# Second layer's value sums with the values as 32-column weights, in a kernel ordered by a planner

## The chip, the cores and the metric

The kernel runs on one core of one Trainium2 chip. The metric is device time in microseconds (us) of one launch. The kernel before takes 1893.77 us (median of 3 runs, 1893.45 to 1894.54).

A core has five engines with queues of their own: PE (matrix multiplication; it reads weights and a moving operand from SBUF and writes PSUM), ACT (ScalarE, here above all exponentials), DVE (VectorE), POOL (GpSimd) and SP (SyncE, here issuing the DMAs). PSUM has 8 banks of 512 f32 columns in 128 partitions.

## The reference

Four layers are applied to x of 2048 tokens by 512 features. Each layer normalizes x, makes Q, K and V with 32 heads of 16 features, attends, and adds the projected result to x. The layers are called first to fourth; in the code they are L = 0 to 3. The first and third (kind A) share one set of weights, the second and fourth (kind B) another.

```python
x = A_x
x = x + _A_ref(_layernorm(x, axis=-1), A_wq, A_wk, A_wv, A_wo, A_beta)
x = x + _B_ref(_layernorm(x, axis=-1), B_wqkv, B_wo)
x = x + _A_ref(_layernorm(x, axis=-1), A_wq, A_wk, A_wv, A_wo, A_beta)
x = x + _B_ref(_layernorm(x, axis=-1), B_wqkv, B_wo)
```

Kind A cuts the tokens into 4 segments of 512. Within a segment it is causal softmax attention; between segments a memory matrix M (a sum of phi(k) v over earlier segments) adds a linear term, mixed by a gate. Kind B is full softmax attention over all 2048 tokens:

```python
scores = jnp.einsum('bhqd,bhkd->bhqk', q, k) * Dh ** (-0.5)
p = _softmax(scores, axis=-1)
o = jnp.einsum('bhqk,bhkd->bhqd', p, v)
```

The softmax runs without subtracting a maximum; the sum of the exponentials comes from a column of ones beside V.

## The kernel before

Work is cut into groups. A group is one layer, one segment of 512 queries (`qseg`), one block of 128 features (`c`, 4 of them) and one parity of heads (`e`), so it holds 4 heads, one in each 32-partition row of the array (r = 0..3); the queries are masked so that only 16 of a row's 32 features count (`qm`). A group's scores come in banks: 128 keys by 512 queries of one head, on a 32-row tile of PE. A full group of kind B has 16 key tiles x 4 heads = 64 banks. A group of kind A has 12 causal ones, worth 10 banks' width.

A unit of work (`unit`, main loop in `attention`) is up to three banks of scores on PE, one ACT instruction that turns them into exp in SBUF (`pT`, line 1349), and the value sums of an earlier unit (`pv`). Units alternate between PSUM banks 0 to 2 and 4 to 6; bank 3 (`DXB`) is for projections and spare scores, bank 7 (`ACC`) is the one accumulator of value sums.

Some banks of kind B go to DVE instead of ACT (`dx_*`): one instruction from PSUM writes a piecewise approximation of exp as 16-bit integers (line 980), three more add constants to it in SBUF (line 1032), and all four copies are summed by PE. So a bank on DVE has four value sums where a bank on ACT has one. `dx_room` decides whether a unit may take some; the copies live in 9 buffers (`dxw`) and in tiles that are free by then (`dx_areas`: four in QA and VA while the second layer's full groups run, and up to 34 in weights, keys and others later).

Value sums have two forms. In the first the exponentials are the weights: 128 keys by 128 queries are loaded, 17 columns of V (16 and the ones) move through, four times for a bank. In the second (`g.fm`) the 17 columns of V are the weights, in a 32-column tile of the array that belongs to the head's row, and the bank's 512 exponentials move through once. `FM` says which groups take the second form (line 264): 1 is the last layer's full groups, 2 all of the last layer, 3 also the second layer's full groups, 4 all of kind B. At the end of a group (`finish`) the first form takes a reciprocal and a product and sends the output to SP's transposing DMA; the second (`finish_fm`) first transposes the accumulator on DVE in 32x32 blocks, then takes reciprocal and product, and for each pair of groups transposes back on DVE. Its temporary tiles are the upper half of KA.

Where keys aren't complete yet, kind B runs partial groups: in the second layer segment 0's queries against each key segment as it comes (32 groups), in the fourth against two segments and again two (`split` cuts the last ones further). Their sums are kept in f32 in free key or value tiles (`accS`).

Everything else (norms, projections, phi, memory, output projections) is a task, a generator that yields between pieces. `ORDER` is each task's priority: for layer pair and segment the keys of task_A, task_phi, task_mem, task_B and task_out. `background` and `bg_one` fit pieces in between units by credits.

The order of all instructions is fixed when the program is built. `Sched` keeps an estimated time for each engine; `Sched.estimate` prices each instruction, a PE instruction by its columns and by how its tile of the array stands to the last twelve. Most class constants of `Builder` (CR_*, DQ, NEAR_*, GAP and so on) are limits on such estimates. `select` chooses the next pair of groups: with `ALT` 1 it goes over to kind B after each pair of the third layer's first two segments. `keep_busy` adds matmuls on zeros where the estimate finds PE too idle.

The start: `setup` issues the input DMAs on SP and 66 warming matmuls; `ln_part` takes mean and variance of four tiles on DVE and an inverse root by two Newton steps; `ln_first` normalizes, transposes on PE and evacuates; then `task_A` projects K and Q of the first block, `select` masks Q from the evacuated copy, and the first unit can run.

Of the kernel before, what the change touches and what calls it, by code (L numbers as in the profile page):

```python
# [4 lines left out]
ACT = mybir.ActivationFunctionType  # L5
ALU = mybir.AluOpType

P = 128
# [4 lines left out]
NCH = 4  # L13
NSEG = 4
SCALE = 0.25
LN_EPS = 1e-5
# [61 lines left out]
class Sched:  # L78

# [142 lines left out]

# [34 lines left out]
class Builder:  # L257
    NPU = 4
    NDX = 9
    FIT, MARGIN = 2, 450  # L260
    PART = 2
    FILL_DVE = 300
    EARLY = 200
    FILL, FILLS = 0.5, 2
# [5 lines left out]
    NKS = 6  # L270
    DX_T, POOL_T, POOL_ON = 430, 2900, 0
# [12 lines left out]
    def alloc(self):  # L284
# [29 lines left out]
        self.lnw = sb("lnw", [P, 2, 4, 4], f32)  # L314
        self.bet = sb("bet", [P, H], bf)
# [68 lines left out]
    HOR = 300  # L384

# [149 lines left out]

    def normalize(self, s, k, i):
# [8 lines left out]
    def ln_first(self, k, slot):  # L545
# [4 lines left out]
        for t, (xn, bx) in enumerate(xns):  # L550
# [3 lines left out]
                    reads=[self.b_x[t], self.b_lnst[k][t], self.b_lnw[k]], writes=[bx])  # L554
        for j in range(2):
# [61 lines left out]
    def task_A(self, L, s):  # L617
# [8 lines left out]
        k = yield from self.ln_part(L, s)  # L626
# [7 lines left out]
        for c in range(NCH):  # L634
            yield from self.proj_fm(self.wA, self.b_wA[1], 512, slot, c, self.KA[:, sl, c, :], self.b_KA[sl][c])
            self.flags.add(("K", L, s, c))
# [316 lines left out]
    FM = 1  # L953
# [758 lines left out]
```

## Time and profile before

| | us |
|---|---|
| median of 3 runs | 1893.77 |
| the profiled execution | 1894.24 |
| its span, first to last instruction | 1892.7 |
| ACT busy | 1798.6 (95%) |
| PE busy, matmuls | 1686.8 (89%) |
| DVE busy | 1535.3 (81%) |
| PE weight loads busy | 891.0 (47%) |
| POOL busy | 277.7 (15%) |
| granted PE clock, mean | 0.994 |

Line numbers are those of the kernel before. PE's instructions nearly all come from one helper (line 402), so a group of them is told by its tiles: `qm,KB` is scores, `VB,pT` value sums of ACT's banks, `VB,dxw` (and QA, VA or others in place of dxw) of DVE's; `128*128` means the first form, `128*17` the second. Where the view gives a releaser ("<-"), that instruction ended the wait. Stages by time: first layer and the second layer's partial groups to 423 us; the second layer's full groups, with the third layer's first two segments in between, to 1084; the third layer's other segments and the fourth's partial groups to 1369; the fourth layer's full groups to 1887.

### The profile page before, as it was taken

The page shows a single profiled execution, that of the slowest core. Times are in us where ns is not written, and L with a number is a line of the kernel's source. Part 1 is how long each engine was busy: PE and PEld are TensorE (multiplying, and loading weights), DVE is VectorE, ACT ScalarE, POOL GpSimd, SP SyncE. Part 2 cuts the span into 40 slices and gives each one's busy share as a digit, 9 for nine tenths or more (in the row PEclk, how much of TensorE's full clock was granted, in tenths as well). Part 3 has the DMA queues.
Part 4 walks back from the last instruction along what each step waited for, and adds up shares of the span by engine and source line. Part 5 has one row for each costly group of instructions (what it writes and reads, how often), then busy time and mean ns, then how long its engine had stood idle before and what let it go on. Part 6 is the DMA issues. An engine that isn't in the chain of part 4 may idle for free.

```text
span 1892.7 us, 64181 instructions
## 1 busy us (share of the span) xinstructions
PE 1686.8 (89%) x27966; PEld 891.0 (47%) x28200; DVE 1535.3 (81%) x3230; ACT 1798.6 (95%) x1642; POOL 277.7 (15%) x646
## 2 busy tenths in 40 slices
PE   7879888899998999999989989899888898889887
PEld 4444445566665556665656656555522222222222
DVE  6566657698797678797778779678999999999996
ACT  6899999899999999999999999999999999999998
POOL 4522333010001110001110050420100000000000
PEclk9999999999999999999999999999999999999999
DMA  5121110000000002000001011010100000000000
GB/s 159 29 35 38 24 18 19 14 14 17 14 8 9 8 8 31 12 19 8 9 8 33 11 24 25 19 19 3 14 12 1 1 11 2 2 1 13 1 1 12
DMA packets 94971, 33.51 MB, mean 18 GB/s; under 512 B 87521, under 2 KB 94177, under 8 KB 94689
## 3 DMA queue, kind: packets, MB, share of 16 engines
q1 hardware_dynamic: 94688, 29.39, 8.0%
q8 instruction: 221, 3.62, 0.8%
q14 instruction: 62, 0.50, 0.1%
HBM read 6.30 MB, written 2.10 MB: 4 GB/s over the span
## 4 chain that ended last, share of the span: by engine, by line
PE 40%; ACT 29%; DVE 16%; issue 12%; DMA 2%; POOL 1%; SPq 0%; ACTq 0%; DVEq 0%; POOLq 0%
PE ps L402 40%; ACT pT L1349 29%; DVE dxw L980 3%; DVE dxw L1032 2%; DMA xT<-xn 1%; DVE ob L1459 1%; DVE lnst L519 1%; DVE x L795 1%; POOL pT L1364 1%; DVE QA L980 0%; DVE rd L1447 0%; DVE VA L1032 0%; DVE wA L980 0%; DVE KB L980 0%; DVE QA L1032 0%
## 5 line engine op out<-in xcount | busy, mean ns | idle before, releaser
L1349 ACT ACTIVATE pT<-ps 128x1536 bf16<-128x1536 f32 (+3 forms) x1605 | 1771.4, 1249 | 70.4 <-PE ps L402 57.6
L402 PE MATMUL ps<-qm,KB 32*128 32x512 bf16 x3584 | 491.6, 386 | 79.5 <-ACT pT L1349 56.5
L1364 POOL TENSOR_SCALAR_AFFINE_SELECT pT<-pT 128x256 bf16<-128x256 bf16 (+2 forms) x529 | 212.8, 421 | 830.4 <-ACT pT L1349 821.0
L402 PEld LDWEIGHTS ps<-VB,pT 128*128 128x128 bf16 x7800 | 256.6, 96 | 162.2 <-issue 107.0
L402 PE MATMUL ps<-VB,pT 128*128 128x51 bf16 (+1 forms) x7800 | 321.9, 187 | 10.7 <-DVE ob L1459 5.5
L980 DVE TENSOR_SCALAR dxw<-ps 128x512 uint16<-128x512 f32 (+1 forms) x309 | 269.8, 876 | 48.9 <-PE ps L402 45.6
L402 PEld LDWEIGHTS ps<-qm,KB 32*128 32x128 bf16 x3584 | 122.2, 91 | 284.0 <-ACT pT L1349 195.2
L402 PE MATMUL ps<-VB,dxw 128*128 128x34 bf16 (+1 forms) x5112 | 212.9, 186 | 0.2 <-issue 0.2
L1032 DVE TENSOR_SCALAR dxw<-dxw 128x1024 uint16<-128x1024 uint16 (+1 forms) x401 | 164.5, 426 | 8.0 <-PE ps L402 5.3
L402 PEld LDWEIGHTS ps<-VB,dxw 128*128 128x128 bf16 x5112 | 167.6, 96 | 5.7 <-issue 3.6
L1266 POOL TENSOR_SCALAR qm<-QB,par 128x512 bf16<-128x512 bf16 x74 | 57.9, 785 | 688.9 <-PE ps L402 560.3
L402 PE MATMUL ps<-VA,pT 128*128 128x51 bf16 (+1 forms) x3036 | 126.7, 188 | 20.0 <-DVE ob L1459 12.6
L402 PEld LDWEIGHTS ps<-VA,pT 128*128 128x128 bf16 x3036 | 100.0, 96 | 77.9 <-POOL pT L1364 42.8
L402 PE MATMUL ps<-qm,KA 32*128 32x128 bf16 (+3 forms) x1024 | 106.1, 303 | 24.0 <-ACT pT L1349 16.1
L402 PE MATMUL ps<-pT,VB 128*17 128x512 bf16 x791 | 126.1, 384 | 1.5 <-DVE KA L1477 0.6
L402 PE MATMUL ps<-qm,QA 32*128 32x512 bf16 x512 | 89.6, 385 | 24.8 <-ACT pT L1349 21.7
L402 PE MATMUL ps<-dxw,VB 128*17 128x512 bf16 x313 | 86.4, 381 | 0.0
L402 PEld LDWEIGHTS ps<-qm,KA 32*128 32x128 bf16 x1024 | 30.5, 91 | 87.7 <-ACT pT L1349 60.9
L402 PE MATMUL ps<-xT,wB 128*128 128x512 bf16 x223 | 63.4, 388 | 5.2 <-issue 2.4
L402 PE MATMUL ps<-xT,wA 128*128 128x512 bf16 x217 | 59.6, 380 | 8.4 <-issue 3.5
L402 PEld LDWEIGHTS ps<-pT,VB 128*17 128x17 bf16 x791 | 29.8, 87 | 76.4 <-issue 66.6
L402 PE MATMUL ps<-wB,zero 128*128 128x512 bf16 x173 | 60.9, 392 | 3.6 <-issue 2.4
(293 smaller groups left out, 2378.8 us busy)
## 6 DMA issues: line engine op xcount, KB each, us to landing
out_dram<-x SPq DMA_DIRECT2D x8, 256.0 KB, 2.1
x<-in_A_x_dram SPq DMA_DIRECT2D x3, 512.0 KB, 9.6
wB<-in_B_wqkv_dram SPq DMA_DIRECT2D x1, 1536.0 KB, 11.8
xT<-xn SPq DMA_TRANSPOSE x60, 2.5
oT<-ob SPq DMA_TRANSPOSE x52, 2.4
x<-in_A_x_dram SPq DMA_DIRECT2D x4, 128.0 KB, 2.1
wA<-in_A_wk_dram SPq DMA_DIRECT2D x1, 512.0 KB, 5.3
wA<-in_A_wq_dram SPq DMA_DIRECT2D x1, 512.0 KB, 6.2
```

Source lines behind the costliest of these rows:

```text
L402: self.sc.add("pe", lambda e: e.matmul(out, lhsT, rhs, start=start, stop=stop, skip_group_check=True), reads=reads, banks=[(bank, "w", all ...
L519: self.op("dve", (lambda i, t: lambda e: e.bn_stats(st[:, k, i, 0:6], self.x[:, t, :]))(i, t), reads=[self.b_x[t]], writes=[bs], ns=690)
L795: self.op("dve", (lambda t, o: lambda e: e.tensor_tensor(self.x[:, t, :], self.x[:, t, :], o, ALU.add))(t, o), reads=[self.b_x[t]], writes ...
L980: self.sc.add("dve", lambda e: e.tensor_scalar(d, o, SCALE * LOG2E * 128, EXP_C, op0=ALU.mult, op1=ALU.add), writes=[w for j in range(k) f ...
L1032: self.op("dve", lambda e: e.tensor_scalar(o, w, d, None, op0=ALU.add), reads=self.b_dxw[b0][:len(ents)], writes=wr, ns=435 if len(ents) = ...
L1266: self.op(eng, (lambda m, q, col: lambda e: e.tensor_scalar(m, q, col, 0.0, op0=ALU.mult, op1=ALU.add))(m, q, col), reads=[bq, self.b_par] ...
L1349: self.sc.add("act", (lambda dst, src: lambda e: e.activation(dst, src, ACT.Exp, scale=SCALE))(dst, src), writes=self.b_pT[slot * 3 + i:sl ...
L1364: self.op("pool", (lambda blk, pat: lambda e: e.affine_select(blk, blk, pattern=pat, compare_op=ALU.is_ge, fill=0.0, base=0, channel_multi ...
L1459: self.op("dve", lambda e: e.tensor_tensor(ob, src[:, :, 0:16], rb, ALU.mult), reads=[br] + bsrc, writes=[self.b_ob[oi][g.e]], bank=bk, al ...
```

## The change

- `FM` goes from 1 to 3: the fourth layer's partial groups and the second layer's full groups take the second form of value sums.
- `Sched.estimate` prices a matmul on another tile shape at 104 ns in place of 100 behind the last one, and a 128-row one behind a 32-row one dearer by 13.
- Most settings have new values; `ALT` 1 becomes 0, so that the third layer's groups go first when they can, ahead of a pair of kind B that was chosen and not begun; `ORDER` is new; `dx_room` reads its limit from four settings in place of two.
- The first norm is split (`ln_start`): three tiles' statistics stay on DVE, one tile's go to ACT (a Copy and a Square with sums), the root is taken by ACT, and a small exponential follows it. Two PSUM memsets leave the setup; the one of `ACC` stands behind the first normalization.
- The first block's Q and K (`first_heads`): Q first, masked on DVE straight from PSUM, K evacuated in two pieces; wq is loaded ahead of wk, and the later x tiles wait on SP for both.

```diff
@@ class Sched, estimate
-            for (a, ar, b, bc, m, at) in self.tiles:
+            for i, (a, ar, b, bc, m, at) in enumerate(self.tiles):
                 if ar < r0 + rows and r0 < ar + a and bc < c0 + cols and c0 < bc + b:
-                    st = max(st, at + m / 2.4 + (4 if (a, b) == (rows, cols) else 100))
+                    after = 104 if (a, b) != (rows, cols) else 5 if cols == 128 else 4
+                    if after == 5 and rows == 128 and 0 < i == len(self.tiles) - 1 and self.tiles[i - 1][0] == 32:
+                        after += 13
+                    st = max(st, at + m / 2.4 + after)
@@ class Builder
-    FIT, MARGIN = 2, 450
-    EARLY = 200
-    DVE_FIN, DX_FIN = 600, 2500
-    EVAC_ACT = 0
-    DX_BANK, DX_LATE, BG_BANK, DVE_LATE, DVE_LATE_LOW = 800, 3000, 200, 1500, 9000000000.0
-    CR_A, CR_B, CR_W, CR_LOW, CARRY, CARRY_W, REST, NEAR, SLACK = 1300, 1500, 1400, 2200, 0, 0, 14, 10, 300
-    ALT3, ALT5, GAP, AHEAD, PE_B, PE_A, PE_LOW, LOW, PAIRS, TAKEN, PAIRS2 = 2, 4, 3, 500, 4, 3, 4, 24, 60, 3, 1
-    DQN, TAKEN_N, REST_N, NEAR_N, NEAR_W = 600, 3, 14, 100, 24
-    DQ, DXS, PVN, PVLATE, PVWAIT, PVHOLE = 2200, 1, 4, 900, 0, 100
-    DMA_STEPS, DMA_LATE = 2, 300
...
+    NPU, NDX, FIT, MARGIN, PART, FILL_DVE, EARLY, FILL = 4, 9, 2, 450, 2, 300, 700, 0.5
+    FILLS, DVE_FIN, DX_FIN, EVAC_ACT, DX_BANK, DX_LATE, BG_BANK, DVE_LATE = 2, 600, 2000, -300, 500, 3000, 200, 1000
+    DVE_LATE_LOW, CR_A, CR_B, CR_W, CR_LOW, CARRY, CARRY_W, REST = 9000000000.0, 1300, 1200, 1400, 1900, 0, 0, 14
+    NEAR, SLACK, ALT3, ALT5, GAP, AHEAD, PE_B, PE_A = 10, 300, 2, 4, 2, 300, 4, 3
+    PE_LOW, LOW, PAIRS, TAKEN, PAIRS2, NKS, DX_T, POOL_T = 5, 24, 60, 3, 1, 6, 430, 2900
+    POOL_ON, DQN, TAKEN_N, REST_N, NEAR_N, NEAR_W, DQ, DXS = 0, 600, 3, 14, 130, 16, 2200, 2
+    PVN, PVLATE, PVWAIT, PVHOLE, DMA_STEPS, DMA_LATE, HOR, PHI = 4, 900, 0, 100, 2, 600, 400, 'kq'
+    CLOSE, FM, NAREA, XDX, NEAR_S, NEAR_E, DX_WAIT, DX_RES = ('proj', 2, 2), 3, 42, 99, 60, 60, 200, 2
+    CHAINS, ALT, ALTS, ALTA = 4, 0, 4, (1, 1, 9, 9)
+    ORDER = [[(2.3, -11.0, 12, 0.9, -10), (3.8, -5.8, 10.4, 20, 9), (19, -2.3, 22, 47.8, 0), (46.0, 39.5, 29.2, 43, 47.1)],
+             [(20.0, 3.3, -3.8, 13, 48.6), (19.4, 44.6, 28.5, 28, 2), (21, 35.0, 8.2, 33, -12), (31, 13.6, 37, 43, -10)]]
...
-    HOR = 300
...
-    FM = 1
...
-    ORDER = [[(2.3, -8.5, 12, 4.9, -10), (10.8, -3.5, 8.4, 25, 4), (21, 25.7, 22, 39.5, 0), (31, 39.5, 44.3, 43, 47.1)],
-             [(1, 1.5, 2, 13, -10), (9.4, 11.5, 12, 28, 0), (21, 21.5, 20, 33, -12), (31, 33.5, 32, 43, -10)]]
-    ALT, ALTS, ALTA = 1, 4, (1, 1, 9, 9)
@@ setup
-                       writes=self.b_x[a:b])
+                       writes=self.b_x[a:b], deps=[self.b_wA[i].last_write for i in (0, 1)] if a == 4 else [])
             if a == 3:
-                for i, nm in ((1, "A_wk"), (0, "A_wq"), (2, "A_wv")):
+                for i, nm in ((0, "A_wq"), (1, "A_wk"), (2, "A_wv")):
...
-        for bk in (ACC, DXB):
-            b = self.banks[bk]
-            b.alloc = -1
-            self.op("dve", (lambda b: lambda e: e.memset(self.ps[:, b.col0:b.col0 + 512], 0.0))(b), bank=b, alloc=-1)
+        pool(lambda e: e.memset(self.eps[:, :], LN_EPS), [self.b_eps])
@@ new
+    def ln_start(self):
...
+        yield [], 0, 3000
+        for i in (0, 1, 3):
+            self.op("dve", (lambda i: lambda e: e.bn_stats(st[:, k, i, 0:6], self.x[:, i, :]))(i), reads=[self.b_x[i]], writes=[bs[i]], ns=690)
+            self.op("dve", (lambda i: lambda e: e.bn_aggr(st[:, k, i, 6:8], st[:, k, i, 0:6]))(i), reads=[bs[i]], writes=[bs[i]], ns=180)
+        nb = st[:, k, 2, 0:1]
+        self.op("act", lambda e: e.activation(junk, self.x[:, 2, :], ACT.Copy, scale=-1 / (512 * root), accum_out=nb),
+                reads=[self.b_x[2]], writes=[bs[2], self.b_pT[0]], ns=620, gap=500)
+        self.op("act", lambda e: e.activation(junk, self.x[:, 2, :], ACT.Square, scale=1 / root, bias=nb, accum_out=st[:, k, 2, 7:8]),
+                reads=[self.b_x[2], bs[2]], writes=[bs[2], self.b_pT[0]], ns=620, gap=500)
...
+        self.op("dve", lambda e: e.tensor_scalar(st[:, k, 2, 6:7], nb, -root, None, op0=ALU.mult), reads=[bs[2]], writes=[bs[2]], ns=165)
+        self.op("act", lambda e: e.activation(v, var, ACT.Sqrt, bias=self.eps[:, 0:1]), reads=bs + [self.b_eps], writes=[bw], ns=230, gap=150)
+        self.op("act", lambda e: e.activation(self.eps[:, 1:2], self.eps[:, 0:1], ACT.Exp), reads=[self.b_eps], writes=[self.b_eps], ns=1500,
+                gap=1400)
+        self.op("dve", lambda e: e.reciprocal(y, v), reads=[bw], writes=[bw], ns=165)
+        return k
@@ ln_first, behind the four normalizations
+        b = self.banks[ACC]
+        b.alloc = -1
+        self.op("dve", lambda e: e.memset(self.ps[:, b.col0:b.col0 + 512], 0.0), bank=b, alloc=-1)
@@ task_A
-        k = yield from self.ln_part(L, s)
+        k = yield from (self.ln_part(L, s) if L or s else self.ln_start())
...
+            if (L, s, c) == (0, 0, 0):
+                self.first_heads(slot)
@@ new
+    def first_heads(self, slot):
+        for i, dst in ((0, self.QA), (1, self.KA)):
...
+            if i:
...
+                self.op("dve", (lambda d, o: lambda e: e.tensor_copy(d, o))(d[:, 0:128], o[:, 0:128]), writes=[self.b_K0], bank=bank, alloc=al, ns=250)
+                self.op("act", (lambda d, o: lambda e: e.activation(d, o, ACT.Copy))(d[:, 128:512], o[:, 128:512]), reads=[self.b_K0], writes=[bk], bank=bank,
+                        alloc=al, ns=500, gap=380)
+            else:
...
+                self.op("dve", (lambda m, o: lambda e: e.tensor_scalar(m, o, col, 0.0, op0=ALU.mult, op1=ALU.add))(m, o), reads=[self.b_par],
+                        writes=[self.b_qm[0]], bank=bank, alloc=al, ns=690)
+                self.op("act", (lambda d, o: lambda e: e.activation(d, o, ACT.Copy))(d, o), writes=[self.b_QA[0][0]], bank=bank, alloc=al,
+                        ns=600, gap=480)
@@ dx_room
-        if self.near < (self.NEAR_W if self.wide else self.NEAR_N) or self.near < self.PAIRS and len(self.dx_pairs) > self.PAIRS2 or not self.dx_build and len(self.dx_bufs) < self.DXS:
+        if self.near < (self.NEAR_N if not self.wide else self.NEAR_W if ("in", 3, 3) in self.flags else self.NEAR_S if ("in", 1, 3) in self.flags else self.NEAR_E) or self.near < self.PAIRS and len(self.dx_pairs) > self.PAIRS2 or not self.dx_build and len(self.dx_bufs) < self.DXS:
```

More of the change, by code (lines that the diff above doesn't have):

```diff
@@ L314, in alloc @@
         self.lnw = sb("lnw", [P, 2, 4, 4], f32)
+        self.eps, self.b_eps = sb("eps", [P, 2], f32), Buf("eps")
+        self.b_K0 = Buf("k0")
         self.bet = sb("bet", [P, H], bf)
@@ L534, in ln_part @@
         return k
+    def ln_start(self):
+        k = self.ring("ln", 2)
+        st, w = self.lnst, self.lnw
+        bs = self.b_lnst[k]
+        junk, root = self.pT[:, 0, 0, :], 512 ** 0.5
+        yield [], 0, 3000
[7 more added lines that the diff above has]
+                reads=[self.b_x[2], bs[2]], writes=[bs[2], self.b_pT[0]], ns=620, gap=500)
+        bw = self.b_lnw[k]
+        v, y, var = w[:, k, 0, :], w[:, k, 1, :], st[:, k, :, 7]
+        self.op("dve", lambda e: e.tensor_scalar(st[:, k, 2, 6:7], nb, -root, None, op0=ALU.mult), reads=[bs[2]], writes=[bs[2]], ns=165)
[4 more added lines that the diff above has]
+        return k
     def normalize(self, s, k, i):
@@ L634, in task_A @@
         for c in range(NCH):
-            yield from self.proj_fm(self.wA, self.b_wA[1], 512, slot, c, self.KA[:, sl, c, :], self.b_KA[sl][c])
-            self.flags.add(("K", L, s, c))
-            yield from self.proj_fm(self.wA, self.b_wA[0], 0, slot, c, self.QA[:, sl, c, :], self.b_QA[sl][c])
-            self.flags.add(("Q", L, s, c))
+            if (L, s, c) == (0, 0, 0):
+                self.first_heads(slot)
+            else:
+                yield from self.proj_fm(self.wA, self.b_wA[1], 512, slot, c, self.KA[:, sl, c, :], self.b_KA[sl][c])
+                self.flags.add(("K", L, s, c))
+                yield from self.proj_fm(self.wA, self.b_wA[0], 0, slot, c, self.QA[:, sl, c, :], self.b_QA[sl][c])
+            self.flags.update([("K", L, s, c), ("Q", L, s, c)])
             if c == 0:
@@ L1308, in unit @@
                 sl = self.aslot(g.L, g.qseg)
-                kt = lambda kb: (self.KA[rows, sl, g.c, kb * 128:(kb + 1) * 128], self.b_KA[sl][g.c])
+                kt = lambda kb: (self.KA[rows, sl, g.c, kb * 128:(kb + 1) * 128], self.b_K0 if (g.L, g.qseg, g.c, kb) == (0, 0, 0, 0) else self.b_KA[sl][g.c])
                 parts = PARTS[what]
```

24 lines of the change are left out of this document (13 added, 11 removed).

## The prediction

> **What bounds the kernel now.** I read first the busy times by stage, cut where the kinds of work change: the second layer's full groups (423 to 1084 us), a run of nothing but third-layer groups (1084 to 1130), the fourth layer's partial groups (1130 to 1369), its full groups (1369 to 1887), and a hole (361 to 371). Columns: stretch, its length, then busy us of PE, PEld, DVE, ACT and POOL.
>
> ```profile
> 361.00:371.00 10.00, 9.41 (x52) 3.90 (x52) 3.73 (x7) 2.15 (x4) 0.69 (x1) 0.68 0.00 0
> 423.00:1084.00 661.00, 614.50 (x12989) 407.02 (x13075) 530.45 (x1128) 632.40 (x577) 61.56 (x151) 0.99 0.08 14
> 1084.00:1130.00 46.00, 39.28 (x652) 22.09 (x660) 35.20 (x85) 44.61 (x48) 27.62 (x68) 1.00 0.19 28
> 1130.00:1369.00 239.00, 218.64 (x4300) 136.47 (x4336) 193.53 (x413) 225.02 (x202) 42.95 (x93) 1.00 0.10 15
> 1369.00:1887.00 518.00, 452.33 (x4359) 122.53 (x4380) 485.33 (x911) 512.93 (x448) 16.42 (x20) 1.00 0.02 5
> ```
>
> The two long stretches do the same job: 24 full groups of 64 score banks each. The first sums values the old way (weights are the 128 columns of exp), the second already with values as 32-column weights. The new way has ACT at 99% and DVE at 94%; the old has ACT at 95.7%, DVE at 80% and PE at 93%. What ACT waits for (the groups of instructions by line, ACT in those two stretches; the last part is idle time and who ended it):
>
> ```profile
> L1349 ACT ACTIVATE pT<-ps 128x1024 bf16<-128x1024 f32 (+3 forms) x567 | 626.2, 1231 | 28.6 <-PE ps L402 22.4 <-POOL pT L1364 1.3 <-issue 0.8
> L1349 ACT ACTIVATE pT<-ps 128x1024 bf16<-128x1024 f32 (+1 forms) x448 | 513.3, 1351 | 2.9 <-PE ps L402 2.5
> ```
>
> 28.6 us of idle against 2.9, most of it ended by PE. So in the second layer PE is what the exponentials wait for, and DVE has 20% free that it can't turn into exponentials, since each of its four copies must pass through PE. In the fourth layer ACT and DVE are both full. The kernel is bound by exponentials that two engines share, with PE in the way in half of the span.
>
> What value sums cost PE is read from starts in the order of time, the old way first (second column: length of the merged stretch):
>
> ```profile
> 453.48 0.37 PE L402 MATMUL ps<-VB,dxw 128*128 128x34 bf16 x8
> 453.69 0.37 PE L402 MATMUL ps<-VB,VA 128*128 128x34 bf16 x8
> 1641.06 0.39 PE L402 MATMUL ps<-pT,VB 128*17 128x512 bf16 x3
> 1641.07 0.39 PE L402 MATMUL ps<-dxw,VB 128*17 128x512 bf16 x1
> 1641.29 0.38 PE L402 MATMUL ps<-QA,VB 128*17 128x512 bf16 x1
> ```
>
> Eight old matmuls start in 0.21 us: 26 ns each, four to a bank, 105 ns. Four new ones stand in the array together and the next four start 0.22 to 0.23 us later: 56 ns a bank if all four columns are filled, 75 if three.
>
> **The change, part by part.**
>
> *Second layer's full groups (FM 1 to 3).* Weight loads of the old sums in 423 to 1084 us give the number of banks:
>
> ```profile
> L402 PEld LDWEIGHTS ps<-VB,pT 128*128 128x128 bf16 x4764 | 158.1, 96 | 106.9 <-issue 76.0 <-DVE ob L1459 9.8 <-ACT pT L1349 2.9
> L402 PEld LDWEIGHTS ps<-VB,dxw 128*128 128x128 bf16 x3819 | 125.2, 96 | 2.9 <-issue 1.6
> L402 PEld LDWEIGHTS ps<-VB,QA 128*128 128x128 bf16 x800 | 30.2, 96 | 1.8 <-issue 0.9
> L402 PEld LDWEIGHTS ps<-VB,VA 128*128 128x128 bf16 x816 | 29.3, 96 | 0.4 <-issue 0.4
> ```
>
> 10199 / 4 = 2550 banks (a DVE bank counts four times). At 30 to 49 ns saved on each, PE gets back 76 to 125 us of its 614.5. With the smaller figure PE needs 538 us; over a stretch of 620 that is 87%, what it has in the fourth layer (452.33 of 518). So I take it that ACT and DVE can run there as they do here. Each closing of a group on DVE gets dearer (rows: first three of 1369 to 1887, last of 423 to 1084):
>
> ```profile
> L1477 DVE STREAM_TRANSPOSE KA<-ps 128x512 f32<-128x512 f32 (+1 forms) x24 | 16.8, 700 | 10.7 <-PE ps L402 10.4
> L1483 DVE TENSOR_TENSOR KA<-KA,rd 128x256 bf16<-128x256 f32 (+1 forms) x24 | 10.1, 419 | 0.8
> L1505 DVE STREAM_TRANSPOSE oT<-KA 128x512 bf16<-128x512 bf16 x11 | 7.7, 704 | 0.1
> L1459 DVE TENSOR_TENSOR ob<-ps,rd 128x256 bf16<-128x256 f32 x39 | 16.6, 424 | 1.3
> ```
>
> 700 + 419 + 704 / 2 (one for two groups) - 424 = 1.05 us, 24 times 25 us; the reciprocal stays. The output's transposing DMA on SP goes away with it (12 of them, off the path: free).
>
> Now the sum for this stretch. Widths of ACT's exponentials (old stretch, then fourth layer), and DVE's first copies and shifts (two views, one line of the kernel each; old stretch, then fourth layer):
>
> ```profile
> L1349 ACT ACTIVATE pT<-ps 128x1536 bf16<-128x1536 f32 x271 | 385.0, 1494 | 13.3 <-PE ps L402 10.6 <-POOL VB L766 0.7 <-ACT pT L1349 0.3
> L1349 ACT ACTIVATE pT<-ps 128x1024 bf16<-128x1024 f32 x247 | 247.0, 1056 | 12.8 <-PE ps L402 10.2 <-issue 0.8 <-POOL pT L1364 0.2
> L1349 ACT ACTIVATE pT<-ps 128x512 bf16<-128x512 f32 x29 | 16.8, 684 | 2.5 <-PE ps L402 1.5 <-POOL pT L1364 0.8
> L1349 ACT ACTIVATE pT<-ps 128x768 bf16<-128x768 f32 x8 | 7.0, 879 | 0.0
> L1349 ACT ACTIVATE pT<-ps 128x256 bf16<-128x256 f32 x12 | 5.2, 432 | 0.0
> L1349 ACT ACTIVATE pT<-ps 128x1536 bf16<-128x1536 f32 x236 | 355.4, 1552 | 1.7 <-PE ps L402 1.5
> L1349 ACT ACTIVATE pT<-ps 128x1024 bf16<-128x1024 f32 x211 | 232.8, 1129 | 1.2 <-PE ps L402 1.0
> ```
>
> ```profile
> 423.00:1084.00 661.00, 217.45 (x259) 0.99 0.08 14
> 1369.00:1887.00 518.00, 242.78 (x221) 1.00 0.02 5
> ```
>
> ```profile
> 423.00:1084.00 661.00, 201.22 (x515) 0.99 0.08 14
> 1369.00:1887.00 518.00, 219.88 (x593) 1.00 0.02 5
> ```
>
> Fourth layer: ACT does 3 x 236 + 2 x 211 = 1130 banks (of 512 columns) in 518 us, 2.18 a us; DVE the other 24 x 64 - 1130 = 406 for 462.7 us, 1.14 us each. Old stretch: ACT does 813 + 494 + 29 + 12 + 6 = 1354 banks, of which 160 are third-layer groups (16 groups of ten banks' width), so DVE does 1536 - 1194 = 342 for 418.7 us, 1.22 each; 530.45 - 418.7 = 112 us of DVE are other work. With both engines as full as in the fourth layer, in T us ACT does 2.18 (T - 8), where 8 us go to its exponentials of the memory part, and DVE (0.937 T - 112 - 25) / 1.2. Together they must do 1536 + 160 = 1696: T = 617, 44 us less. That is the far end (50 with DVE at 1.14). Near end: PE didn't hold anything up, and the 25 us of DVE are 21 banks more for both engines, 7 us lost.
>
> Taken off the 44: the first two segments of the third layer now run unmixed (below), 4.4 us; and projections still cut into PE here, which the fourth layer doesn't have, some 6 us. I take -34, near the far end, because the fourth layer's rows are the same groups in the new form.
>
> *Third layer ahead of the second (ALT 1 to 0, ORDER).* Its groups have no DVE share, so a run of them leaves DVE to other work: 35.20 of 46 us in 1084 to 1130, 7.9 below 94%. Two more such runs lose 16 us of DVE, 13 banks, 4.4 us (counted above).
>
> *Fourth layer's partial groups*, also in the new form: eight last closings at +1.05 us and 22 partial sums of 512 columns in place of 272 (at most 0.33 us more each, by the 700 ns row in proportion), 16 us of DVE or 4 us lost if nothing else moves; far end, ACT's 14 us of idle shrinks to the fourth layer's share, 9 us won. PE is at 91% there too: -5.
>
> *First norm split.* Four rows of DVE in order of time, ACT's table load and its first exponential:
>
> ```profile
> 0.80 1.28 ACT L564 ACT_TABLE_LOAD   x1 [0.80 <-PEq L1697]
> 5.07 0.66 DVE L519 BATCH_NORM_STATS2 lnst<-x 128x6 f32<-128x512 bf16 x1
> 5.86 0.66 DVE L519 BATCH_NORM_STATS2 lnst<-x 128x6 f32<-128x512 bf16 x1
> 6.77 0.17 DVE L526 TENSOR_SCALAR lnw<-lnst 128x4 f32<-128x4 f32 x1
> 8.37 0.73 DVE L552 TENSOR_SCALAR xn<-x,lnst,lnw 128x512 bf16<-128x512 bf16 x2
> 14.48 1.45 ACT L1349 ACTIVATE pT<-ps 128x1536 bf16<-128x1536 f32 x1 [0.88 <-PE ps L402]
> ```
>
> One tile's statistics leave DVE (0.8 us), the 1.6 us of Newton steps become a square root on ACT between two short DVE steps (about 0.8 saved), the memsets ahead of the first statistics go (up to 0.5; one of them returns behind the fourth normalization, hidden by the transposes). The first scores are made from Q and a 128-column piece of K (about 0.7). Against it, ACT must load tables for the root and load exp again; the second load, 1.28 us by the row, ends after the first transposes are ready, about 0.6 late. Sum -2.2; between +1 (loads in the path) and -3. The input loads put behind wq and wk, and wo, wqkv and wo of the other layers behind them on SP, come some 5 us later; their first users are at 30 us and after: free. The Trainium skill (ScalarE: Activation LUTs, What ACT_TABLE_LOAD costs) puts a switch of sets at about 2.66 us with its drain; by that the gain here would be 0.9. The one load in this trace is shorter.
>
> *Settings and planner costs* add no instruction. Where they can show is the hole at 361 to 371 us, with ACT busy 2.15 of 10: 7.8 us if it closes, 4 lost if it grows by half: -3. Elsewhere 0, give or take 2.
>
> Sum: -34 - 5 - 2.2 - 3 = -44, on the profiled execution's 1894.24 us (span 1892.7; 0.5 above the median of the runs): **1850 us**.
>
> **Rivals.**
>
> *PE was not the bound.* PE's busy time is modelled. The Trainium skill (Perfetto Trace Analysis, Identifying the Most-Contended Engine) calls it a bad measure and asks for the share of weight loads. By weight loads, 407.02 of 661, PE is at 62%, and relief would buy nothing: +7 for DVE, -5.2 from start and hole, about 1896. Against it: the starts above follow one another without room, and 22.4 us of ACT's idle end on PE. Chance 0.05.
>
> *ACT gains, DVE doesn't.* The second layer has 13 buffers for DVE's copies (rows with dxw, QA, VA only), the fourth up to 43. If buffers, not PE, held DVE at its 418.7 us less 25, it does 321 banks, ACT 1375: 8 + 1375 / 2.18 = 638 us, 23 won; with the start and nothing from the partial groups or the hole, 1869 to 1873. For it: DVE's 80%. Against: a buffer comes free when PE has read it, and PE reads sooner. Chance 0.20.
>
> *Everything as full as in the fourth layer*: -50 - 9 - 3 - 8, about 1825. Chance 0.08.
>
> *Closings hold the accumulator* (the other side). There is one accumulator bank; the next group's sums wait until the last DVE copies of this one are summed and transposed, now with one transposing buffer, and later copies with few buffers. Now the worst such wait is small (waits in 423 to 1084: us, times, longest):
>
> ```profile
> PEld ps L402 <- DVE ob L1459: 9.8, 16, 1.1
> ```
>
> It decides from 44 / 24 = 1.8 us of ACT at each of 24 closings, more than one exponential of 1.45 us. At 2.5 us each: +60 - 44, about 1910. Chance 0.12.
>
> **How the numbers follow.** Forecast 0.55 (its own range 1836 to 1866), rivals 0.05, 0.20, 0.08, 0.12. About 0.2% (4 us) is what a measurement can tell from no change. Faster 0.84, same 0.04, slower 0.12. The range leaves out the closings' case, half of the first rival and a little below the full case: 1820 to 1889.
>
> **What would show it.** Right: the stretch of second-layer full groups shortens by some 34 us; sums there appear as 128*17 by 512 columns; ACT's idle before PE falls from 22 us to under 10; DVE rises above 88%; first exponential near 12.3 us. Wrong: DVE still near 80% there (second rival); PE idle ended by the transposes with over 1 us a time (the last one); a hole as at 361 us somewhere else, where third-layer groups now come early and the second layer's work runs out.

## The result and the profile after

The changed kernel takes 1852.93 us (median of 4 runs, 1849.94 to 1856.26) against 1894.03 us before: a ratio of 0.978, with a 95% interval of 0.9767 to 0.9792. The profiled execution took 1852.87 us, its span is 1850.3. In the kernel after, PE's helper is line 396, ACT's exponentials are line 1388, DVE's first copies line 1019, its shifts line 1070 and the transposes of the accumulator line 1516.

Busy time of each engine over the span, after (the table ahead of the prediction has those of before):

```profile
PE 1633.2 (88%) x17868; PEld 584.5 (32%) x18082; DVE 1546.9 (84%) x3332; ACT 1803.5 (97%) x1689; POOL 288.3 (16%) x651
```

ACT was idle 1892.7 - 1798.6 = 94.1 us before and is idle 1850.3 - 1803.5 = 46.8 us now. It works 5 us more and waits 47 us less; that is the whole 42 us of span. Over the whole program DVE did not take over more exponentials. Its first copies and shifts over the whole span, before and after:

```profile
0.00:1900.00 1900.00, 565.68 (x603) 0.99 0.09 18
0.00:1900.00 1900.00, 522.96 (x1371) 0.99 0.09 18
```

```profile
0.00:1900.00 1900.00, 569.76 (x695) 0.99 0.07 16
0.00:1900.00 1900.00, 514.74 (x1353) 0.99 0.07 16
```

Together 1088.6 and 1084.5 us, nearly the same; by the widths of the first copies that is 890 banks before and 885 after. The chain of work that ended last, as shares of the span, before and after:

```profile
PE 40%; ACT 29%; DVE 16%; issue 12%; DMA 2%; POOL 1%; SPq 0%; ACTq 0%; DVEq 0%; POOLq 0%
```

```profile
ACT 41%; PE 30%; issue 15%; DVE 12%; POOL 1%; DMA 1%; SPq 0%; ACTq 0%; DVEq 0%
```

PE led the chain before, ACT leads it now. By stage (columns as in the prediction: stretch, length, then busy us of PE, PEld, DVE, ACT, POOL, and the granted clock). The third layer's first three segments lie inside the second row of each, so that the rows hold equal work. Before; its last stage, from 1369, is quoted in the prediction:

```profile
0.00:423.00 423.00, 360.57 (x5687) 202.64 (x5756) 288.20 (x691) 382.42 (x370) 129.19 (x314) 0.99 0.18 39
423.00:1125.00 702.00, 649.09 (x13527) 425.68 (x13621) 561.22 (x1201) 672.01 (x620) 89.18 (x219) 0.99 0.08 15
1125.00:1369.00 244.00, 223.34 (x4407) 139.90 (x4446) 197.97 (x424) 230.02 (x206) 42.95 (x93) 1.00 0.10 15
```

After; the fifth row is a stretch inside the first:

```profile
0.00:412.00 412.00, 356.29 (x5562) 200.12 (x5634) 274.04 (x653) 389.82 (x381) 130.61 (x314) 0.98 0.17 40
412.00:1085.00 673.00, 613.35 (x5983) 196.81 (x6063) 590.02 (x1340) 663.87 (x643) 94.26 (x225) 0.99 0.07 13
1085.00:1328.00 243.00, 213.60 (x1959) 67.44 (x1990) 186.64 (x391) 235.71 (x214) 44.68 (x92) 0.99 0.05 10
1328.00:1845.00 517.00, 448.75 (x4364) 119.91 (x4394) 493.83 (x946) 512.92 (x452) 18.80 (x20) 1.00 0.01 4
...
341.00:411.00 70.00, 62.24 (x1224) 38.67 (x1227) 52.69 (x104) 67.54 (x58) 8.43 (x11) 1.00 0.05 10
```

The first stage gives 11 us, the second layer's full groups 29, the fourth layer's partial groups 1, its full groups 1. In the full groups PE is busy 613 of 673 us (91%) and ACT 98.6%. ACT's exponentials from there to the fourth layer's first finished partial group (422 to 1137 us before, 412 to 1096 after), as a group by line (last part: idle time before them and who ended it), before and after:

```profile
L1349 ACT ACTIVATE pT<-ps 128x1536 bf16<-128x1536 f32 (+4 forms) x620 | 677.0, 1217 | 30.1 <-PE ps L402 23.3 <-POOL pT L1364 1.4 <-issue 0.8
```

```profile
L1388 ACT ACTIVATE pT<-ps 128x1024 bf16<-128x1024 f32 (+4 forms) x643 | 668.2, 1165 | 9.2 <-PE ps L396 4.0 <-POOL pT L1403 2.2
```

Idle ended by PE fell from 23.3 to 4.0 us. PE's weight loads now wait for ACT far more than before. Waits of PE's weight loads (us, times, longest) in 423 to 1125 us before and in 412 to 1085 us after:

```profile
PEld ps L402 <- ACT pT L1349: 53.9, 129, 1.2
```

```profile
PEld ps L396 <- ACT pT L1388: 184.9, 399, 1.1
...
PEld ps L396 <- DVE KA L1516: 5.2, 14, 0.6
```

### The profile page after: what moved, and what is told of

Same layout as the page of the kernel before. It is cut to its first block, busy times and chain, and to the rows that moved or that the text cites. A ratio compares the mean times of both kernels' runs of the same rounds, so it can differ in the third digit from the quotient of the medians.

```text
span 1850.3 us, 44068 instructions
## 1 busy us (share of the span) xinstructions
PE 1633.2 (88%) x17868; PEld 584.5 (32%) x18082; DVE 1546.9 (84%) x3332; ACT 1803.5 (97%) x1689; POOL 288.3 (16%) x651
## 4 chain that ended last, share of the span: by engine, by line
ACT 41%; PE 30%; issue 15%; DVE 12%; POOL 1%; DMA 1%; SPq 0%; ACTq 0%; DVEq 0%
ACT pT L1388 41%; PE ps L396 30%; DVE dxw L1019 2%; DVE dxw L1070 2%; POOL pT L1403 1%; DVE VB L423 0%; DVE x L837 0%; DVE KA L1516 0%; DVE lnst L510 0%; DMA xT<-xn 0%; ACT amem L623 0%; DVE QA L1070 0%; DVE QA L1019 0%; SPq L430 0%; DVE VA L1070 0%
## 5 line engine op out<-in xcount | busy, mean ns | idle before, releaser
L1388 ACT ACTIVATE pT<-ps 128x1024 bf16<-128x1024 f32 (+3 forms) x1642 | 1772.1, 1225 | 33.4 <-PE ps L396 23.7
L396 PE MATMUL ps<-pT,VB 128*17 128x512 bf16 x2274 | 365.7, 384 | 11.4 <-ACT pT L1388 5.6
L396 PE MATMUL ps<-dxw,VB 128*17 128x512 bf16 x1521 | 316.8, 381 | 0.1
L1019 DVE TENSOR_SCALAR dxw<-ps 128x512 uint16<-128x512 f32 (+1 forms) x376 | 276.9, 748 | 16.3 <-PE ps L396 14.5
L1070 DVE TENSOR_SCALAR dxw<-dxw 128x1024 uint16<-128x1024 uint16 x441 | 177.4, 419 | 3.5 <-PE ps L396 0.6
L396 PEld LDWEIGHTS ps<-pT,VB 128*17 128x17 bf16 x2274 | 85.8, 87 | 242.7 <-issue 206.6
L396 PE MATMUL ps<-qm,KA 32*128 32x512 bf16 (+3 forms) x1024 | 107.2, 307 | 30.6 <-ACT pT L1388 24.9
L396 PE MATMUL ps<-qm,QA 32*128 32x512 bf16 x512 | 89.4, 384 | 23.3 <-ACT pT L1388 21.8
L396 PE MATMUL ps<-pT,VA 128*17 128x512 bf16 x470 | 78.6, 384 | 6.6 <-ACT pT L1388 5.8
L396 PE MATMUL ps<-VA,VB 128*17 128x512 bf16 x275 | 79.2, 381 | 0.0
L396 PE MATMUL ps<-VB,pT 128*128 128x51 bf16 (+1 forms) x1868 | 73.1, 186 | 2.3 <-ACT pT L1388 1.8
L396 PE MATMUL ps<-QA,VB 128*17 128x512 bf16 x241 | 73.2, 381 | 0.0
L396 PEld LDWEIGHTS ps<-VB,pT 128*128 128x128 bf16 x1868 | 60.6, 96 | 31.9 <-issue 16.7
```

What stands on the lines that cost most here:

```text
L396: self.sc.add("pe", lambda e: e.matmul(out, lhsT, rhs, start=start, stop=stop, skip_group_check=True), reads=reads, banks=[(bank, "w", all ...
L1019: self.sc.add("dve", lambda e: e.tensor_scalar(d, o, SCALE * LOG2E * 128, EXP_C, op0=ALU.mult, op1=ALU.add), writes=[w for j in range(k) f ...
L1070: self.op("dve", lambda e: e.tensor_scalar(o, w, d, None, op0=ALU.add), reads=self.b_dxw[b0][:len(ents)], writes=wr, ns=435 if len(ents) = ...
L1388: self.sc.add("act", (lambda dst, src: lambda e: e.activation(dst, src, ACT.Exp, scale=SCALE))(dst, src), writes=self.b_pT[slot * 3 + i:sl ...
```

## The experiments

The first theory is the prediction's: the form of the value sums takes PE out of ACT's way, and order and settings are worth little. The rivals are that PE was not what ACT waited for, and, added for these runs, that order and settings make the gain. Two questions are put: which part carries the 41 us, and by what. Every kernel was timed beside the kernel before on the same chip.

**1. Part of PE's work left out of the kernel before.** In the second layer's full groups the sums of two of the four query blocks are not issued after each head's first bank; the order of everything else stays.

```diff
-                    not g.started, g.left == 0, [bp, bv], bank, g.acc, n=52 if n == 3 else 50)
-            g.started.add(0)
+                    not g.started, g.left == 0, [bp, bv], bank, g.acc,
+                    "drop" if g.L == 1 and g.first and g.last and q0 in (128, 256) and (q0, r) in g.started ...)
+            g.started |= {0, (q0, r)}
...
+            if op.name == "drop" and not op.emit:
+                continue
```

> The kernel before with the same order on every engine, but two of each bank's four value sums in the second layer's full groups are left out (the query blocks 1 and 2, after the first bank of each head), so the outputs for those queries are wrong. PE gets back about 2500 banks x 52 ns = 130 us there; DVE's share of banks stays as planned. Theory that PE holds the exponentials up there: ACT falls to its own time, 1354 banks / 2.18 a us + 8 = 629 in place of 661 us, total about 1862 (1856 to 1872). Rival that PE was not the bound: 1892 to 1895.

1907.75 us, ratio 1.0061 (1.0039 to 1.0084): less work on PE, and slower. Busy time by stretch (the clock is the third number from the end), without the sums, and before:

```profile
423.00:1150.00 727.00, 645.36 (x8975) 340.62 (x8975) 571.73 (x1229) 685.68 (x630) 89.89 (x220) 0.82 0.08 14
903.00:923.00 20.00, 17.50 (x271) 10.08 (x272) 15.08 (x30) 19.26 (x17) 0.00 (x0) 0.67 0.01 2
```

```profile
422.00:1137.00 715.00, 661.62 (x13792) 434.26 (x13893) 573.50 (x1228) 684.90 (x630) 89.87 (x220) 0.99 0.08 15
```

The clock fell to 0.82 over the stage: with the order fixed beforehand, nothing took the place of the matmuls left out. The run settles nothing about PE as the bound; it shows only that this much of PE's work cannot be taken out of this order without the clock falling.

**2. The form alone, on the old order and settings.**

```diff
-    FM = 1
+    FM = 3
```

> The kernel before with FM 3 alone. Theory that the form of the value sums carries the gain: 1894 less 25 to 34 for the second layer's full groups, less 0 to 5 for the fourth layer's partial groups: 1856 to 1869. Rival that the new settings and the order carry it: 1884 or more.

1903.74 us, ratio 1.004 (1.0024 to 1.0056): the form alone loses 7.8 us. ACT in the same stage:

```profile
L1349 ACT ACTIVATE pT<-ps 128x1536 bf16<-128x1536 f32 (+4 forms) x617 | 670.1, 1220 | 30.0 <-PE ps L402 25.1 <-POOL pT L1364 2.5 <-issue 1.2
```

PE's weight loads fall as they should (586.4 us over the span, 891.0 before), and ACT still waits 25.1 us for PE. Yet PE had room: of its 631.74 busy us in that stage of 709, 55.12 are matmuls on zeros, and from 422 to 1120 us its weight loads wait 206.6 us for ACT (53.9 before, in 423 to 1125):

```profile
PEld ps L402 <- ACT pT L1349: 206.6, 379, 1.6
```

So idle time of ACT that ends on PE does not by itself show that PE lacks time: here each waits for the other, and PE's relief left that idle as it was. By stage, in the traces, the second layer's full groups are 6 us shorter than before (the table below), and the fourth layer's partial groups, which took the new form too, 9 us longer. The new form in full groups alone, on the old settings, was not tried.

**3. Everything but the form.**

```diff
-    CLOSE, FM, ... = ('proj', 2, 2), 3, ...
+    CLOSE, FM, ... = ('proj', 2, 2), 1, ...
```

> The changed kernel with FM 1 again, all else new. Theory that the form carries the gain: the 29 us of the second layer's full groups are lost, 1876 to 1888. Rival that settings and order carry it: 1853 to 1865.

1897.94 us, ratio 1.0013 (0.9998 to 1.0027): order, settings, planner's prices and start together gain nothing measurable without the form. ACT's row of the stage and the stage's busy times:

```profile
L1388 ACT ACTIVATE pT<-ps 128x1024 bf16<-128x1024 f32 (+3 forms) x625 | 688.6, 1248 | 23.8 <-PE ps L396 20.6 <-POOL pT L1403 1.4 <-issue 0.7
```

```profile
413.00:1132.00 719.00, 676.16 (x13513) 427.90 (x13513) 538.02 (x1176) 695.17 (x636) 93.51 (x226) 0.99 0.08 15
```

With the same settings and another form, 20.6 us of ACT's idle end on PE instead of 4.0, PE is at 94%, and by the widths of its first copies DVE makes 308 banks there instead of 357, which ACT has to make (1818.7 us busy over the span instead of 1803.5). That fits the prediction's picture of PE in the way of both engines, but it is not the form's doing alone: the kernel before, with the same old form, has DVE make 346 banks. Under the new settings and order the old form gets fewer banks onto DVE than under the old ones.

The kernels before and after and runs 2 and 3 are a square: neither half gains alone, both together gain 2.2%. So the next runs look for what makes the form pay.

**4. The old order of layers and ORDER in the kernel after.**

```diff
-    ..., ALT, ... = 4, 0, ...
-    ORDER = [... new ...]
+    ..., ALT, ... = 4, 1, ...
+    ORDER = [... old ...]
```

> The changed kernel with ALT 1 and the old ORDER. If the hole at 361 to 371 us and its neighbours were closed by the order of tasks, the 8 to 10 us won ahead of 412 us are lost: 1861 to 1867. If other settings closed it, 1850 to 1857. The unmixed third-layer groups were priced at 4 us of loss: without them up to 4 us less than either.

1873.49 us, ratio 0.9882 (0.9867 to 0.9896): 21 us of the gain are gone.

**5. The alternation of layers alone.**

```diff
-    ..., ALT, ... = 4, 0, ...
+    ..., ALT, ... = 4, 1, ...
```

> The changed kernel with ALT 1 alone (its ORDER kept). Theory that mixing third-layer groups (sums in the old form) with second-layer groups in the new form costs ACT: idle near third-layer groups goes from 6 us back to 20 or more, total 1865 to 1876. Rival that the priorities in ORDER made the 20 us that ALT 1 with the old ORDER cost: 1849 to 1858.

1880.02 us, ratio 0.9923 (0.9907 to 0.994): 27 us of the gain are gone, 6.5 more than in run 4, which undoes this and ORDER. ACT in the stage:

```profile
L1388 ACT ACTIVATE pT<-ps 128x1024 bf16<-128x1024 f32 (+4 forms) x633 | 667.5, 1198 | 20.6 <-PE ps L396 18.2 <-ACT pT L1388 0.2
```

Mixing the third layer's groups in between brings back 14 us of idle ended by PE, although the sums have the new form.

**6. Form and unmixed layers on the old settings.**

```diff
-    FM = 1
-    ALT, ALTS, ALTA = 1, 4, (1, 1, 9, 9)
+    FM = 3
+    ALT, ALTS, ALTA = 0, 4, (1, 1, 9, 9)
```

> The kernel before with FM 3 and ALT 0, all else old. Theory that form and unmixed third-layer groups belong together: 12 to 20 us less than FM 3 alone (1904), 1884 to 1892. Rival that ALT 0 helps only with the other new settings: 1900 to 1908.

1888.64 us, ratio 0.9967 (0.9953 to 0.998). Not mixing is worth 15 us to the form here too (1903.74 in run 2); the form with it gains 0.3%, not 2.2%. The step of 15 us is no larger than what runs 9 and 11 below lose by small edits.

**7. The new form in full groups only**, so that the fourth layer's partial groups keep the old one.

```diff
-        self.fm = kind == "B" and Builder.FM >= (1 if L == 3 and first and last else 2 if L == 3 else 3 ...)
+        self.fm = kind == "B" and first and last
```

> The changed kernel with the new form for full groups only (second and fourth layer); the fourth layer's partial groups sum in the old form. If the form won 5 us there, as forecast: 1856 to 1860. If its dearer closings (16 us of DVE) took all that PE gave: 1849 to 1855. If they took more: under 1848.

1860.23 us, ratio 0.9815 (0.9799 to 0.9831): 7.3 us more than the kernel after, 3 of them in the fourth layer's partial groups.

**8. The old start**: the old first norm, first heads, order of loads and memsets.

```diff
-        k = yield from (self.ln_part(L, s) if L or s else self.ln_start())
+        k = yield from self.ln_part(L, s)
...
-            if (L, s, c) == (0, 0, 0):
-                self.first_heads(slot)
```

> The changed kernel with the old start (norm on DVE alone, Newton steps, K first, old order of loads). By the two first exponentials (14.48 and 13.54 us) 1 us is lost: 1852 to 1856. Rival that the start, through the planner, also made the 10 us that are won ahead of 412 us: 1861 to 1865.

1855.02 us, ratio 0.9789 (0.9774 to 0.9804): 2.1 us more than the kernel after, within the spread of that kernel's own runs. The first exponential starts at 14.47 us. ACT's and DVE's rows of the kernel after, in order of time (start, length; in brackets the wait):

```profile
5.42 0.19 ACT L541 ACTIVATION_READ_ACCUMULATOR pT<-x,lnst 128x1 f32 x1
5.62 1.28 ACT L546 ACT_TABLE_LOAD   x1
6.92 0.30 ACT L546 ACTIVATE lnw<-lnst,eps 128x4 f32<-128x4 f32 x1
7.24 1.28 ACT L547 ACT_TABLE_LOAD   x1
```

```profile
5.64 0.15 DVE L545 TENSOR_SCALAR lnst<-lnst 128x1 f32<-128x1 f32 x1
7.25 0.18 DVE L549 RECIPROCAL lnw<-lnw 128x4 f32<-128x4 f32 x1 [1.46 <-ACT lnw L546]
```

The table for the root is loaded between the statistics and the root, with DVE waiting 1.46 us behind it. The first exponential starts at 13.54 us in place of 14.48 before. An earlier load of that table was not tried.

**9. The planner's old prices.**

```diff
-                    after = 104 if (a, b) != (rows, cols) else 5 if cols == 128 else 4
-                    if after == 5 and rows == 128 and 0 < i == len(self.tiles) - 1 and self.tiles[i - 1][0] == 32:
-                        after += 13
-                    st = max(st, at + m / 2.4 + after)
+                    st = max(st, at + m / 2.4 + (4 if (a, b) == (rows, cols) else 100))
```

> The changed kernel with the old TensorE costs in the planner (100 ns on another tile shape, 4 otherwise). Priced at 0, give or take 2, in the prediction: 1851 to 1857. Rival that the settings were found for the new costs and the plan loses its fit with the old: 1860 or more, with the loss spread over all stages.

1868.43 us, ratio 0.9858 (0.9841 to 0.9876): 15.5 us more than the kernel after, for prices of 100 and 4 ns in place of 104 and 5 (and 13 in one case).

**10. All other settings old**: ALT 0, the new ORDER, form, prices and start stay.

```diff
-    ... HOR ... = ..., 400, ...
-    ... NEAR_S, NEAR_E ... = ..., 60, 60, ...
+    ... every setting of the kernel before but FM, ALT and ORDER ...
+    NEAR_S = NEAR_E = 24
```

> The changed kernel with its form, order (ALT 0, new ORDER), start and TensorE costs, but every other setting as before. If form and unmixed order carry the gain, only the hole ahead of 412 us comes back (9 us): 1860 to 1866. If the settings are part of what cuts ACT's idle: 1870 or more, as with FM 3 and ALT 0 on the old kernel (1889).

1899.3 us, ratio 1.0021 (1.0007 to 1.0036): the whole gain is gone, and 5 us with it.

**11. One setting old**, the limit below which a unit takes no banks for DVE in the second layer.

```diff
-    ... NEAR_S, NEAR_E ... = ..., 60, 60, ...
+    ... NEAR_S, NEAR_E ... = ..., 24, 24, ...
```

> The changed kernel with the limit of banks ahead below which DVE takes none back at 24 (from 60) until the fourth layer's inputs are whole. DVE's banks in the fourth layer's partial groups fell from 93 to 79 with the change. If that limit ate the gain there: 90 banks or more again, and the stage 3 to 6 us shorter, total 1847 to 1851. If DVE's banks there delay the projections the stage waits for: 1853 to 1862.

1869.57 us, ratio 0.9859 (0.9835 to 0.9884): 16.6 us more than the kernel after; in its trace the second layer's full groups take 12 us longer.

**12. No matmuls on zeros while a third-layer group runs**, on the kernel of run 5, to see whether these matmuls are what ACT waits for in mixed stretches.

```diff
     def keep_busy(self):
+        if any(h.kind == "A" for h in self.sel):
+            return
```

> The changed kernel with ALT 1 (1880) and no zero matmuls while a third-layer group is chosen. ACT's idle near third-layer groups is 15 us there against 6 with ALT 0, 12 of it beside zero matmuls. If those, queued ahead of the next scores on PE, cost it: idle back to 6 to 8 us, total 1868 to 1874, if the clock holds. If the mixing itself costs, or the clock gate closes (half clock over 60 us): 1878 or more.

1932.48 us, ratio 1.02 (1.0185 to 1.0215), 52 us more than run 5. Its stage, and that of run 5:

```profile
419.00:1165.00 746.00, 636.27 (x5945) 200.16 (x5999) 590.44 (x1286) 678.49 (x635) 88.28 (x218) 0.89 0.05 10
```

```profile
413.00:1110.00 697.00, 618.44 (x6059) 194.25 (x6130) 593.10 (x1299) 676.41 (x646) 91.41 (x223) 0.99 0.06 11
```

The clock fell to 0.89, so the question of the run stays open.

**The runs side by side.** ACT's idle time from the second layer's last partial group to the fourth layer's last, sorted by whether a masking instruction of POOL (only third-layer groups have one there) lies within 4 us; worked out from each trace, as is the length of the full groups' stage, taken from closing to closing. Each trace is one execution; those of runs 6 and 9 lie 6 us above and 5 us below their medians.

| kernel | median | full groups' stage | idle near the third layer | idle elsewhere |
|---|---|---|---|---|
| before | 1894.0 | 715.5 | 16.2 | 27.5 |
| form alone (2) | 1903.7 | 709.2 | 27.3 | 18.0 |
| form, unmixed, old settings (6) | 1888.6 | 702.9 | 16.1 | 17.3 |
| all but the form (3) | 1897.9 | 719.5 | 11.2 | 25.6 |
| after, mixed (5) | 1880.0 | 696.6 | 15.0 | 17.9 |
| after, mixed, old ORDER (4) | 1873.5 | 699.0 | 25.0 | 8.6 |
| after, other settings old (10) | 1899.3 | 705.8 | 14.5 | 15.9 |
| after, one setting old (11) | 1869.6 | 697.0 | 10.9 | 17.4 |
| after, old prices (9) | 1868.4 | 691.9 | 12.0 | 12.3 |
| after | 1852.9 | 684.8 | 7.1 | 9.3 |

Where only the form differs, the last column falls: 27.5 to 18.0 with the old settings, 25.6 to 9.3 with the new. With the old settings and mixed layers the form raises the column before it, 16.2 to 27.3; unmixed layers take that back to 16.1, and with the new settings both are down. The columns do not order the runs by time: run 4 has 25.0 near the third layer and run 5 only 15.0, and run 4 is the faster one. Nor does the form fix what ACT waits for on PE: with the new form in the second layer's full groups, idle ended by PE there is 4.0 us in the kernel after and 11.6, 14.1, 18.2 and 25.1 in runs 9, 11, 5 and 2. The plan decides how much of PE's relief reaches ACT; how it does was not isolated.

How far can one undo be read? Each edit makes the planner order the whole program anew. Runs 9 and 11 undo things for which no row of the trace of before gives a price, and cost 15.5 and 16.6 us. That fits settings which were chosen for this exact program, so that any step away from it is likely to lose; no run shows it directly. So in this kernel an undo that costs under some 15 us says little of its part. The form (45 us, run 3), the alternation (27, run 5) and the settings together (46, run 10) stand clear of that; run 7's 7 us and run 8's 2 us do not. The parts also add up to more than the whole, as they would if each undo loses some of this fit.

## Why the prediction was right, and where not

The total was right (1850 against 1853), and its largest term nearly so. Smaller terms were wrong in both directions and met in the sum, which is luck: full and partial groups gave 30 us, not 39, and the first stage 11, not 5. And the account of the largest term was incomplete: it made the form alone carry it. Of the signs named for being right, the sums' shape and ACT's idle before PE (4.0 us) came; DVE reached 87.7% in the full groups, not over 88, and the first exponential 13.54 us, not 12.3.

*The second layer's full groups, -34.* Measured -29 for equal work. With the new settings on both sides the form shortens this stage from 719.5 (run 3) to 684.8 us, and PE ends 4.0 us of ACT's idle in place of 20.6. With the old settings on both sides it shortens it from 715.5 to 709.2 (run 2), and the idle ended by PE does not fall (23.3, then 25.1), though PE had room. So the term was taken to belong to the form by itself, and that step failed: as a whole run 2 gives +7.8 us. The term holds only with the order and the settings that came with it, and that PE's time is what ACT waited for is shown only as far as run 3 goes. Against the kernel before, DVE gained less than the sum held: 357 banks in place of 346, at 88% (590.02 of 673) and not 94%. PE's relief was smaller too: matmuls on zeros take 21.67 us of the stage before and 33.05 after, and without them PE's busy time falls by 47 us, where the prediction had 76 to 125 (the ends of matmuls are modelled, so this is rough). Most of the stage's 31 us between the two groups by line is idle of ACT that went away, 30.1 - 9.2 = 20.9 us; 677.0 - 668.2 = 8.8 us are less work on ACT.

*Third layer ahead, 4.4 lost.* Wrong in sign. The step priced only DVE's free time in unmixed runs. Undoing it costs 27 us with the new settings (run 5; 21 with the old ORDER beside it, run 4), and adding it to the form on the old ones gains 15 (run 6). Part of this is in the table: idle near third-layer groups falls from 27.3 (run 2) to 16.1 us (run 6), and from 15.0 (run 5) to 7.1. Of run 5's 27 us, 12 lie in the full groups' stage; what the rest is was not looked into. Why mixed groups leave ACT waiting for PE was not settled; run 12 was meant to tell.

*Settings and prices, -3, elsewhere 0 give or take 2.* The hole at 361 to 371 us did close (67.54 of 70 us busy in 341 to 411), and the first stage as a whole gave 11 us, about 1 of them by the start. "Elsewhere 0" is the step that failed: the settings together are worth 46 us to the final program (run 10), and nothing without the form (run 3). "Adds no instruction" was no reason for a price of nothing, since settings place every instruction. Which settings do it stays open.

*Fourth layer's partial groups, -5.* The stage gave 1. DVE makes 79 banks there in place of 93, and ACT works 235.71 in place of 230.02 us. PE's weight loads fell there (139.90 to 67.44 us). What keeps the stage from getting shorter stays open; by run 7 the new form is worth 3 us in it.

*First norm, -2.2.* 0.94 at the first exponential. Three rows of the kernel after (first normalization, first scores, first exponential), and the first scores before:

```profile
7.47 0.73 DVE L568 TENSOR_SCALAR xn<-x,lnst,lnw 128x512 bf16<-128x512 bf16 x2
12.45 1.05 PE L396 MATMUL ps<-qm,KA 32*128 32x512 bf16 x3 [0.39 <-DVE KA L680]
13.54 1.45 ACT L1388 ACTIVATE pT<-ps 128x1536 bf16<-128x1536 f32 x1 [0.48 <-PE ps L396]
```

```profile
14.04 0.39 PE L402 MATMUL ps<-qm,KA 32*128 32x512 bf16 x3 [1.08 <-DVE qm L1266]
```

The statistics end 1.22 us earlier, as the sum had it (0.8 and up to 0.5). The term that failed is the root in place of the Newton steps: its table load was taken as hidden, but it starts when ACT's own statistics end, and DVE waits for it, so that the step costs 0.32 us more where 0.8 less was forecast. The first normalization starts 0.90 us earlier, at 7.47 in place of 8.37. Behind it two more terms missed and cancel. The second load delays nothing where 0.6 was forecast: ACT's copy of the transposes starts 1.22 us behind the first normalization in both kernels. The scores' 0.7 don't arrive: the first score starts 0.69 us earlier, counted from the first projection, but the first exponential takes three banks. Before, their scores start together; now the second and the third wait for ACT's two copies, of Q and of the rest of K. Each load in this trace takes 1.28 us, and the root starts 0.02 us after its load. The Trainium skill's figure of about 2.66 us for a switch (ScalarE: Activation LUTs, What ACT_TABLE_LOAD costs) gave 0.9 in the prediction (2.2 less 2.66 - 1.28 is 0.8) and came out near by luck: no row shows its drain.

*The rivals.* "PE was not the bound" gave 1896, and the result refutes the time; that relief of PE buys nothing is refuted with the new settings (run 3, 45 us), while with the old it did buy nothing (run 2). By weight loads PE was at 62% in that stage before and at 60% in run 3 (427.90 of 719), and relief of PE bought nothing from the one and 45 us from the other. The Trainium skill (Perfetto Trace Analysis, Identifying the Most-Contended Engine) gives this share, beside the share of peak arithmetic, as the measure of TensorE's distance from its peak; it does not tell these two cases apart. The idle time ended by PE, 23.3 and 20.6 us, tells them apart no better. "ACT gains, DVE doesn't" is half true: over the whole span DVE's exponentials stayed at about 1085 us, but in the second layer's full groups DVE made 357 banks, not 321, and the total is 16 to 20 us below that rival's. "Everything as full as in the fourth layer" did not come: DVE stayed at 88% there. "Closings hold the accumulator" needed 1.8 us at each of 24 closings; the waits for the accumulator's transposes are 5.2 us in 14 waits, the longest 0.6.

## What to carry to other kernels

In a kernel whose order is planned, a cheaper form on one engine may pay only when the plan is made anew with it, as here: test form and plan as a square of four runs, not one after the other. Idle time that ends on an engine does not yet show that the engine lacks time: look also at what that engine waits for. Before a small undo is read as a part's worth, undo something that should cost nothing, and take what it costs as the least that such runs can tell. Read the critical engine's idle time by what it stands next to: here the split by neighbouring layer showed that the form alone helped in one place and hurt in another, where the total moved by 0.4%.

## What the runs showed of the hardware

Two kernels with less work on PE ran at a lower granted clock and were slower. Without nearly half of the second layer's old sums the granted clock was 0.82 over the stage, and 0.67 in 20 us in which PE still shows 17.50 us busy; by the trace's clock records, 283 us of that run were at half clock, in steps of about 3.4 us, against 25 before. Without the matmuls on zeros it was 205 us, against 37 with them, and the run took 52 us longer; there the planner ordered the program anew as well, so not all of the 52 need be the clock's. The Trainium skill (TensorE: Matmul & The Clock Gate, Part 1) gives half and full rate as the only two and a window of 3413 ns; the steps agree. It also advises against idle gaps of more than about 3 us (Why this matters for your kernels): in the first of these runs PE's longest gap in the stage was 1.57 us by the trace's modelled ends, and the clock fell nevertheless, so staying under that figure was not enough here. In the second one gap reached 13.8 us. How much work PE needs to keep the full clock no run here shows.
